# A TensorE loop of 15 rounds, wo in 256 KB pieces, and one VectorE chunk in a decode attention block

## Chip, core, metric

One Trainium2 chip, one core. The metric is the time of one execution on the device in microseconds, as the median over several executions. The kernel before took 670.3 us (median of three runs, 668.88 to 671.2) when the prediction was made. All runs quoted here were in the same (fast) state.

## The reference, cut to what matters

One decode step for two sequences: a layer norm, a q projection, attention over a cache of 8192 keys for 32 heads of 128, the output projection, a residual, and a small ReGLU feed-forward.

```python
B, Sq, D, Hq, Hkv, Sk, Dh, F = 2, 1, 512, 32, 32, 8192, 128, 1376   # all bf16
q = (layernorm(x) @ wq)                            # wq 512 x 4096
scores = einsum("bhqd,bhkd->bhqk", q, k_cache) * Dh ** -0.5
o = einsum("bhqk,bhkd->bhqd", softmax(scores), v_cache)
h = x + o.reshape(B, 1, 4096) @ wo                 # wo 4096 x 512
# h + (relu(g) * u) @ W_down, g and u from layernorm(h) @ W_gate, W_up
```

K and V together are 268 MB, all inputs 281 MB. Nothing is used twice, so the kernel is a stream of loads with arithmetic hidden beside it.

## The kernel before

The 64 (sequence, head) rows are treated as 32 pairs of heads. A pair has one K tile and one V tile of 4 MB. Four slots of 4 MB hold K of two pairs and V of two pairs. For each pair:

- VectorE scores 96 of the 128 key columns that a partition holds, in two chunks of 48: one product, four halving additions, one reduction;
- TensorE transposes the other 32 columns in four groups, ScalarE copies them out of PSUM, and TensorE multiplies them with q;
- ScalarE exponentiates; TensorE multiplies the probabilities with V.

Every engine's program is written out: TensorE's holds 3,187 matmul calls. In the profile a matmul and its weight load are two instructions, and 37 fp32 products stand there as two matmuls each (lines 408 and 319 of the kernel before: 64 and 10 matmuls for 32 and 5 calls), hence 3,224 of each.

```python
# loads: all are issued from one queue (SP), in this order
nc.sync.dma_start(X[:], A_wq.rearrange("(p c) n -> p (c n)", c=DC)).then_inc(sem_wq, 16)
t_k[0] = load(0, slot[0][:], kv(A_k_cache, 0))
# ... v0, k1, v1 into slots 1 to 3
sp.wait(t_q)                                   # X is free once q is there
nc.sync.dma_start(X[:].rearrange("p (h n) -> p h n", n=D),
                  A_wo.rearrange("(h d) n -> d h n", d=128)).then_inc(sem_wo, 16)   # 4 MB in 1 KB rows

for p in range(NP):                            # 32 pairs, cut
    for c in range(NCH):                       # two chunks of 48 columns
        j0, j1 = parts[1 + c]
        dve.wait(t_k[p], t_q_b)
        t_dm = dve.run(nc.vector.tensor_tensor(
            out=prod[:, 0:jc, :], in0=k_t[:, j0:j1, :], in1=qv, op=ALU.mult))
        # ... four tensor_tensor additions (128 -> 8 columns) and a tensor_reduce
        if c == 0:
            pe.wait(t_k[p])
            for g in range(ng):                # four groups of eight key columns
                # ... nc.tensor.transpose x4, ScalarE copy to kT, score_group(p, g - 1)
    if p + 2 < NP:
        sp.wait(t_dm, t_pt[p * NG + ng - 1])   # K slot read by VectorE and by TensorE
        t_k[p + 2] = load(s, slot[s][:], kv(A_k_cache, p + 2))
    if p < NP - 2:
        pv(p)                                  # 32 matmuls, 32 x 512 each
        # ... load_v(p + 2) after pv(p)
```

The softmax here doesn't subtract the row's maximum and nothing guards it: scores larger than these inputs give would overflow.

## Time and profile before

| | |
|---|---|
| time | 670.3 us, profiled execution 669.11 us, span 667.3 us |
| HBM read | 281 MB, 421 GB/s over the span |
| DMA engines | data queue 98.8% of 16 engines' span |
| VectorE / TensorE / ScalarE | 74% / 48% / 32% busy |
| last weights landed | 661.8 us |

These are lines of the page: busy time and share of each engine, the DMA's busy share in 40 slices (tenths), the DMA queues (packets, MB, share of sixteen engines), and the chain of waits that ended last.

```profile
span 667.3 us, 7705 instructions
...
PE 320.9 (48%) x3224; PEld 198.0 (30%) x3224; DVE 490.5 (74%) x433; ACT 211.4 (32%) x535; POOL 5.8 (1%) x17
...
DMA  9999999999999999999999999999999999999995
...
q1 hardware_dynamic: 15600, 281.06, 98.8%
q8 instruction: 25, 0.41, 0.3%
q14 instruction: 9, 0.07, 0.0%
...
DMA 68%; DVE 22%; PE 5%; ACT 3%; issue 1%; SPq 0%; DVEq 0%; ACTq 0%
```

The DMA row has a 9 in every slice but the last. The queues q8 and q14 do not carry data: they carry instructions, 25 packets in q8 (of 16 KB each, by their sizes in the trace) and 9 in q14 within the span (of 8 KB). They are 0.3% of the DMA's time.

Two groups of instructions (line, engine, operation, output<-input, count, then busy us and mean ns, then idle time before them and its cause): the product of 48 columns and the transposes, both waiting for K.

```profile
L433 DVE TENSOR_TENSOR prod<-slot,q_b 128x6144 bf16<-128x6144 bf16 (+1 forms) x64 | 212.8, 3324 | 127.1 <-DMA slot<-in_A_k_cache_dram 124.3
...
L458 PE MATMUL T<-ident_f,slot 128*128 128x128 f32 x528 | 134.7, 422 | 65.4 <-DMA slot<-in_A_k_cache_dram 65.3
```

DMA issues (operation and count, KB each, median us from issue to landing):

```profile
slot<-in_A_k_cache_dram SPq DMA_DIRECT2D x32, 4096.0 KB, 27.7
slot<-in_A_v_cache_dram SPq DMA_DIRECT2D x31, 4096.0 KB, 30.8
...
X<-in_A_wo_dram SPq DMA_DIRECT2D x1, 4096.0 KB, 49.2
```

A load lands 28 to 31 us after its issue, but in the middle of the run the 4 MB loads land 9.7 us apart (300.46, 310.19, 319.90 us). So two loads or more stand in the queue at any time, and an earlier issue alone should gain nothing (tested in e6: K issued 4.9 us sooner, 666.05 us against 665.86).

The end, from the timeline (start us, duration us, engine, line, operation, what it wrote and read, count), cut to the residual sum, the last products and the issue of the output:

```profile
657.49 0.17 DVE L529 TENSOR_TENSOR hb<-W,xlT 128x8 bf16<-128x8 f32 x1 [0.52 <-PE W L352]
...
661.63 1.47 PE L595 MATMUL O<-hd,slot 128*128 128x2 bf16 x40
...
662.96 0.27 PE L595 MATMUL O<-hd,wd_last 96*128 96x2 bf16 x4
...
663.73 0.39 SPq L607 DMA_DIRECT2D out_dram<-o_c  x1
```

and the two W_down loads with their issue and landing times:

```profile
L510 SPq DMA_DIRECT2D slot<-in_B_W_down_dram x2: 434/6450/12466, 634.6 to 635.1; - x2
...
DMA to landing us min/median/max: 25.8/26.3/26.7
```

The second W_down piece was issued at 635.1 us and landed 26.7 us later, at 661.8 us; the last product ended at 663.2 and the span at 667.3.

One more reading is not on the page. Every load here raises its semaphore 16 times, and the trace keeps the time of every increment, but not what made it. They are read here as one from each of the sixteen DMA engines, which the trace does not name. Read so, the spread between the first and the last says how far the engines have drifted apart:

| load of the kernel before, landed at | spread of its 16 increments |
|---|---|
| 24.0 us (K of pair 0) | 1.9 us |
| 230.9 us | 2.0 us |
| 271.2 us | 3.5 us |
| 465.6 us | 3.6 us |
| 505.9 us | 5.0 us |
| 655.1 us (W_up) | 5.1 us |

The 9th instruction packet of q8 started at 262.0 us and the 17th at 499.0 us: just before each step.

The single increments show more. After each of the first eight q8 packets one more of the sixteen comes late: in the loads that landed at 24.0, 43.5, 85.2, 114.4, 143.5, 172.7, 201.8 and 230.9 us, each the first to land after a packet, 1, 2, 3 and so on to 8 increments come 1.7 us or more after the first one. After the 9th packet one of those already late comes 3.5 us after the first, and after the 17th one comes 5.0 us after it. Six increments stay within 0.7 us of the first to the last W_up load, 4.5 to 5.1 us ahead of the latest.

### The profile page before, as it was taken

The numbers are of one execution on the slowest core, as the hardware profiler recorded it, in microseconds if no ns is written. First come the engines' busy times: TensorE is split into PE (matmuls) and PEld (weight loads), VectorE is DVE, ScalarE is ACT, GpSimd is POOL, SyncE is SP. The second block draws the span as 40 slices with busy tenths as digits, with TensorE's granted clock in tenths as the row PEclk, the third lists the DMA queues.
The fourth block names the chain that finished last, engine by engine and source line by source line (L and its number), as shares of the span: only waits on it lengthen the run. The fifth ranks groups of instructions, "written<-read, shape, count | busy, mean of one in ns | idle before, by whom it ended". The sixth has DMA issues, their size and how long they took to land.

```text
span 667.3 us, 7705 instructions
## 1 busy us (share of the span) xinstructions
PE 320.9 (48%) x3224; PEld 198.0 (30%) x3224; DVE 490.5 (74%) x433; ACT 211.4 (32%) x535; POOL 5.8 (1%) x17
## 2 busy tenths in 40 slices
PE   2552353545445434635435553553446564355456
PEld 2330221322223212423213332331224432142336
DVE  1775477797778779777778977777895977788781
ACT  0621222333331323333223333322334142243360
POOL 3000000000000000000000000000000000000000
PEclk9855555555555555555555555555555555555576
DMA  9999999999999999999999999999999999999995
GB/s 377 439 427 364 431 433 423 438 429 431 428 435 428 428 431 437 428 429 430 435 430 431 426 434 428 438 423 432 433 434 426 431 432 428 432 429 434 423 427 203
DMA packets 15638, 281.54 MB, mean 422 GB/s; under 512 B 1426, under 2 KB 6900, under 8 KB 6900
## 3 DMA queue, kind: packets, MB, share of 16 engines
q1 hardware_dynamic: 15600, 281.06, 98.8%
q8 instruction: 25, 0.41, 0.3%
q14 instruction: 9, 0.07, 0.0%
q10 hardware_dynamic: 4, 0.00, 0.0%
HBM read 281.05 MB, written 0.00 MB: 421 GB/s over the span
## 4 chain that ended last, share of the span: by engine, by line
DMA 68%; DVE 22%; PE 5%; ACT 3%; issue 1%; SPq 0%; DVEq 0%; ACTq 0%
DMA slot<-in_A_k_cache_dram 68%; DVE prod L433 14%; DVE tb L441 5%; DVE prod L441 3%; PE T L458 2%; ACT kT L465 2%; DVE scores L448 1%; PE Ob L408 1%; PE S L294 1%; ACT e L304 1%; PE O L392 0%; ACT os_sb L402 0%; PE O L375 0%; PE S L551 0%; PE Ob L319 0%
## 5 line engine op out<-in xcount | busy, mean ns | idle before, releaser
L433 DVE TENSOR_TENSOR prod<-slot,q_b 128x6144 bf16<-128x6144 bf16 (+1 forms) x64 | 212.8, 3324 | 127.1 <-DMA slot<-in_A_k_cache_dram 124.3
L375 PE MATMUL O<-slot,e 128*32 128x512 bf16 x992 | 115.8, 619 | 209.4 <-ACT e L304 133.0
L465 ACT ACTIVATE kT<-T 128x1024 bf16<-128x1024 bf16 x132 | 131.2, 1022 | 165.6 <-PE T L458 161.8
L458 PE MATMUL T<-ident_f,slot 128*128 128x128 f32 x528 | 134.7, 422 | 65.4 <-DMA slot<-in_A_k_cache_dram 65.3
L441 DVE TENSOR_TENSOR tb<-prod 128x3072 bf16<-128x3072 bf16 (+2 forms) x128 | 146.9, 1147 | 4.4
L458 PEld LDWEIGHTS T<-ident_f,slot 128*128 128x128 f32 x528 | 97.2, 217 | 91.9 <-DMA slot<-in_A_k_cache_dram 90.2
L375 PEld LDWEIGHTS O<-slot,e 128*32 128x32 bf16 x992 | 28.4, 127 | 271.8 <-ACT e L304 159.6
L304 ACT ACTIVATE e<-scores 64x48 bf16<-64x48 f32 (+1 forms) x128 | 32.6, 255 | 239.0 <-DVE scores L448 237.2
L441 DVE TENSOR_TENSOR prod<-tb 128x1536 bf16<-128x1536 bf16 (+2 forms) x128 | 83.6, 653 | 4.4
L294 PE MATMUL S<-q,kT 128*128 128x4 bf16 x1056 | 50.1, 169 | 39.2 <-ACT kT L465 39.0
L294 PEld LDWEIGHTS S<-q,kT 128*128 128x128 bf16 x1056 | 43.7, 108 | 69.2 <-ACT kT L465 67.2
L448 DVE TENSOR_REDUCE scores<-prod 128x48 f32<-128x384 bf16 (+1 forms) x64 | 35.1, 549 | 2.3
L304 ACT ACTIVATION_READ_ACCUMULATOR e<-scores 64x1 f32 x128 | 23.6, 185 | 0.0
L408 PE MATMUL Ob<-sel,os_sb 128*128 128x8 f32 x64 | 14.2, 351 | 11.7 <-ACT os_sb L402 11.7
L304 ACT ACTIVATE e<-S 64x32 bf16<-64x32 f32 (+1 forms) x64 | 13.0, 204 | 15.3 <-PE S L294 14.5
L408 PEld LDWEIGHTS Ob<-sel,os_sb 128*128 128x128 f32 x64 | 13.4, 311 | 12.7 <-ACT os_sb L402 12.7
L304 ACT ACTIVATION_READ_ACCUMULATOR e<-S 64x1 f32 x64 | 12.8, 201 | 0.7
L269 ACT ACTIVATE q_b<-O 128x512 bf16<-128x512 f32 x8 | 4.3, 595 | 16.5 <-PE O L264 16.5
L225 DVE CAST qT<-W 128x64 bf16<-128x64 f32 x1 | 0.2, 225 | 11.0 <-PE W L220 11.0
L327 DVE TENSOR_REDUCE zr<-Ob 128x16 f32<-128x48 f32 (+1 forms) x4 | 0.8, 206 | 10.1 <-PE Ob L319 10.1
L220 PE MATMUL W<-xlT,X 128*128 128x2 bf16 x128 | 3.6, 165 | 7.6 <-DMA X<-in_A_wq_dram 7.6
L220 PEld LDWEIGHTS W<-xlT,X 128*128 128x128 bf16 x128 | 3.5, 104 | 7.7 <-DMA X<-in_A_wq_dram 7.7
(69 smaller groups left out, 65.8 us busy)
## 6 DMA issues: line engine op xcount, KB each, us to landing
slot<-in_A_k_cache_dram SPq DMA_DIRECT2D x32, 4096.0 KB, 27.7
slot<-in_A_v_cache_dram SPq DMA_DIRECT2D x31, 4096.0 KB, 30.8
X<-in_A_wq_dram SPq DMA_DIRECT2D x1, 4096.0 KB, 12.2
X<-in_A_wo_dram SPq DMA_DIRECT2D x1, 4096.0 KB, 49.2
slot<-in_A_v_cache_dram SPq DMA_DIRECT2D x2, 2048.0 KB, 28.2
slot<-in_B_W_up_dram SPq DMA_DIRECT2D x1, 1376.0 KB, 21.4
slot<-in_B_W_gate_dram SPq DMA_DIRECT2D x1, 1376.0 KB, 24.3
slot<-in_B_W_down_dram SPq DMA_DIRECT2D x1, 768.0 KB, 25.8
```

The costliest lines, as they stand in the source:

```text
L220: i = nc.tensor.matmul(Wp[:, h * B:(h + 1) * B], lhsT=wq[:, c, h * Dh:(h + 1) * Dh], rhs=lT[:, c * B:(c + 1) * B], start=(c == 0), stop=(c ...
L269: t_cp[m] = act.run(nc.scalar.activation(out=q_b[:, m * 512:(m + 1) * 512], in_=Op[m % 2][:], func=ACT.Copy))
L294: i = nc.tensor.matmul(Sp[p % 2][:, 2 * jj:2 * jj + 4], lhsT=kv_[:, k, r, :], rhs=q2[:, p, r, :], start=(r == 0), stop=(r == 1))
L304: t = act.run(nc.scalar.activation(out=e_t[qd][q, j0 // VJ:j1 // VJ, 8 * qd:8 * qd + 8].rearrange("p g (j a) -> p g j a", a=2)[:, :, :, a] ...
L327: dve.run(nc.vector.tensor_reduce(out=zr[:, 2 * p0:2 * p1], in_=zbank(k)[:, zcol(k):zcol(k) + n * (NCH + 1)].rearrange("p (n k) -> p n k", ...
L375: i = nc.tensor.matmul(Op[gr % 2][c:c + 32, :], lhsT=e_t[qd][:, j // VJ, :], rhs=v_t[:, j:j + VJ, :].rearrange("p j d -> p (j d)"), start= ...
L408: i = nc.tensor.matmul(Ob[:, 2 * p0:2 * p0 + 2 * PG], lhsT=os_sb[:, jj * Dh:(jj + 1) * Dh], rhs=sel[:, 2 * PG * jj:2 * PG * jj + 2 * PG], ...
L433: t_dm = dve.run(nc.vector.tensor_tensor(out=prod[:, 0:jc, :], in0=k_t[:, j0:j1, :], in1=qv, op=ALU.mult))
L441: dve.run(nc.vector.tensor_tensor(out=o, in0=cur[:, :, 0:half], in1=cur[:, :, half:w], op=ALU.add))
L448: t_s = dve.run(nc.vector.tensor_reduce(out=sc[:, 0:jc], in_=cur, axis=AX.X, op=ALU.add))
L458: i = nc.tensor.transpose(Tp[n % 2][:, k * 128:(k + 1) * 128], k_t[:, j:j + 2, :].rearrange("p j d -> p (j d)").bitcast(F32), ident_f[:])
L465: t_ev[n] = act.run(nc.scalar.activation(out=kT[n % 2][:], in_=Tp[n % 2][:].bitcast(BF16), func=ACT.Copy))
```

## The change

Intent: make TensorE's program short. The 30 first pairs become 15 rounds of a loop whose body handles two pairs with fixed addresses and fixed semaphore counts. That has consequences: q of the pair has to be copied to a fixed place (by POOL), wo must be at a fixed place too and so comes as 256 KB for each round, the X tile of 4 MB goes (wq uses slot 3), and the freed memory holds VectorE's working tiles for all its 96 columns in one chunk. The diff, cut to its core:

```diff
-    NCH = 2
-    JC = (J - NG * GT) // NCH
+    JC = J - NG * GT
-    PG = 4
+    PG = 2
+    NI = NP // 2 - 1
-        X = sb("X", [128, H * D], BF16)
+        wo_cur = sb("wo_cur", [128, 2 * D], BF16)
+        wo_last = sb("wo_last", [128, 2 * D], BF16)
+        q2c = [sb(f"q2c{i}", [128, 2, 4], BF16) for i in range(2)]
 ... cut ...
+                with nc.Fori(0, NI, engines=OrderedEngineSet([nc.tensor.engine])):
+                    jd = split(0)[1]
+                    k_part(body, 0, 0, ((g2p, 1),))
+                    collect(body, 6)
+                    pv(body, 0, ((jd, J, ((v2p, 1), (a2p, 5))), (0, jd, ((a2p, 7),))))
+                    k_part(body, 1, 7, ((g2p, 2),))
+                    nc.tensor.wait_ge(d2p, 1)
+                    nc.tensor.wait_ge(v2p, 2)
+                    o_proj(body, wo_cur, 0, B)
+                    nc.tensor.sem_inc(d2p, -1)
+                    pv(body, 1, ((jd, J, ((v2p, 3), (a2p, 12))), (0, jd, ((a2p, EV),))))
+                    z_sum(body, Ob)
+                    nc.tensor.sem_inc(g2p, -2)
+                    nc.tensor.sem_inc(v2p, -3)
+                    nc.tensor.sem_inc(a2p, -EV)
 ... cut: two pairs and the last products written out after the loop ...
+                    if p < P0:
+                        nc.gpsimd.wait_ge(slot_sem[s], 16 * (g + 1))
+                    nc.gpsimd.tensor_copy(out=q2c[p % 2][:], in_=q2[:, p]).then_inc(g2p, 1)
 ... cut ...
-                    for c in range(NCH):
-                        j0, j1 = parts[1 + c]
-                        dve.wait(t_k[p], t_q_b)
+                    dve.wait((slot_sem[s], 16 * (g + 1)), t_q_b)
+                    t_dm[p] = dve.run(nc.vector.tensor_tensor(
+                        out=prod[:, 0:jd, :], in0=k_t[:, 0:jd, :], in1=qv, op=ALU.mult))
 ... cut ...
+                    if p % 2 == 1 and 1 <= g < NI:
+                        sp.wait(tok("om", g))
+                        load_wo(wo_cur, g, sem_wo)
```

In the built programs TensorE has 6,415 instructions before and 1,468 after: 357 ahead of the loop, 355 in its body, 752 after it, and four at the program's two ends (a matmul call counted as two, fp32 doublings not counted). The 25 packets for 6,415 instructions are about 257 a packet; the blocks of 256 instructions in the prediction are this estimate.

## The prediction

> **What bounds the kernel.** The DMA. In the page's slices the sixteen DMA engines are 90% or more busy from the first slice to the last but one; the queue table gives 98.8% to the data queue, 281 MB at 422 GB/s. In the chain of waits 68% is the K loads. VectorE is 74% busy, TensorE 48%; both wait for K in every 19.4 us pair. At the end, the last weight piece lands at 661.8 us and the span ends 5.5 us later.
>
> **Where DMA time is lost.** The trace holds the sixteen completion increments of every load. Their spread is 1.9 us on the first K load, 2.0 at 230 us, 3.6 from 270 us, 5.1 from 510 us: six engines end 4.5 to 5 us before the slowest. The steps follow the instruction queue: 25 packets of 16 KB, one about every 28 us, 1.0 to 1.1 us each; the 9th and the 17th make the steps. So TensorE's instruction blocks seem to be fetched over eight of the engines in turn, each fetch setting its engine back about 1.5 us, and a load lands with its slowest engine. That costs about 4.4 us at the end.
>
> **What the change does.**
> 1. The TensorE loop: 3,224 matmuls with as many weight loads become about 900 pairs of program text. The body is about 365 instructions, two blocks. [...] nothing in this trace shows a branch. If the blocks stay, some 5 to 8 fetches are left, the slowest engine gains about 3 us. If each round fetches two or three blocks again, there are 35 to 50: spread over eight engines about 0 to +4 us, on the same two or three engines about +17 us (estimate: 15 x 1.45 less 4.4). [...]
> 2. wo in pieces: same 1 KB packets (348 GB/s between 54 and 64 us, against about 437), so the same loss, spread out: 0 to +0.5.
> 3. One 96-column chunk: the product takes about 6.6 us instead of two of 3.36; K slots come free about 4.5 us sooner, V slots at the same time (probabilities after about 15 us either way). The queue holds two loads already: about 0.
> 4. Tail: the last pair's P.V uses wide matmuls; the copy, selection and scaling add about 2.5 us after it but 128 narrow matmuls go. Attention ends 1 to 2 us earlier, hidden behind the weights' landing.
>
> **On the critical path:** only the fetches (item 1) and the tail's DMA end. Likely sum: -3 + 0.5 = about -2.5 us.
>
> **Predicted: 667.5 us, 80% range 663 to 682.** Faster by over 2%: 0.02; within 2%: 0.84; slower by over 2%: 0.14.
>
> **What would show it.** Instruction packets fall from 25 to under 10; the spread of the last loads' increments falls from 5.1 to about 2 to 3 us; the last weight lands near 659 us and the span ends 5 to 6 us later; DMA busy stays about 99%; K issue to landing grows from 27.7 to about 32 us.
>
> **What would make it wrong.** More instruction packets than before (refetch each round), worst if they sit on few engines: spread over 10 us, pair period over 19.6 us. Or gaps in the DMA slices, if slots come free late (the even pair's start after the branch, or the relay through POOL).

"If the blocks stay" is an assumption. About -3 us for item 1 under that assumption, at most +0.5 for item 2 and about 0 for items 3 and 4 come to -2.5 us. From 670.3 us that is 667.8; the 667.5 is 0.3 us lower, and the text does not say why.

## The result, and the profile after

The changed kernel takes **665.86 us** (median of four runs, 665.75 to 666.0) against 670.75 us for the kernel before in the same comparison (median of four, 668.88 to 671.74). The ratio is 0.993, 95% interval 0.9908 to 0.9953: the same at 2%, but clearly 0.7% faster. Ratios here are the mean time of one kernel's fast runs over that of the other's of the same rounds, so not quite the ratio of the medians. The measured time lies inside the forecast range; the gain was 4.9 us between the medians instead of the forecast 2.8 from 670.3.

The same lines of the page:

```profile
span 664.0 us, 7589 instructions
...
PE 339.3 (51%) x3223; PEld 220.8 (33%) x3223; DVE 465.7 (70%) x275; ACT 198.5 (30%) x416; POOL 194.1 (29%) x48
...
DMA  9999999999999999999999999999999999999996
...
q1 hardware_dynamic: 15840, 281.06, 99.2%
q8 instruction: 5, 0.08, 0.0%
q14 instruction: 7, 0.06, 0.0%
...
DMA 71%; DVE 26%; PE 1%; ACT 0%; issue 0%; SPq 0%; DVEq 0%
```

The instruction packets of TensorE went from 25 to 5, as forecast, and q14 from 9 to 7. The data queue's share rose to 99.2%: the same bytes in less time. The chain now holds W_down's landing (5% in the full listing), so the end is closer to the data.

The groups that answer to those of before, and the costliest one, which is new:

```profile
L455 POOL COPY q2c<-q 128x8 bf16<-128x8 bf16 x32 | 190.3, 5947 | 417.2 <-DMA slot<-in_A_k_cache_dram 359.6
L466 DVE TENSOR_TENSOR prod<-slot,q_b 128x12288 bf16<-128x12288 bf16 (+1 forms) x32 | 207.7, 6492 | 130.4 <-DMA slot<-in_A_k_cache_dram 128.8
L325 PE MATMUL T<-ident_f,slot 128*128 128x128 f32 x528 | 136.5, 426 | 219.3 <-POOL q2c L455 217.0
```

POOL's copy of eight numbers a partition takes 5.9 us on average, and TensorE's transposes now wait for it (217.0 of their 219.3 us of idle time) instead of for K.

The issues:

```profile
slot<-in_A_k_cache_dram SPq DMA_DIRECT2D x32, 4096.0 KB, 28.1
slot<-in_A_v_cache_dram SPq DMA_DIRECT2D x31, 4096.0 KB, 31.6
...
wo_cur<-in_A_wo_dram SPq DMA_DIRECT2D x15, 256.0 KB, 27.1
```

K's time from issue to landing hardly moved (27.7 to 28.1 us); the forecast had said about 32. The middle of the run shows why, in the timeline around one pair, whose K landed at 321.42 us:

```profile
321.45 6.56 DVE L466 TENSOR_TENSOR prod<-slot,q_b 128x12288 bf16<-128x12288 bf16 x1 [2.55 <-DMA slot<-in_A_k_cache_dram]
321.55 6.51 POOL L455 COPY q2c<-q 128x8 bf16<-128x8 bf16 x1 [12.94 <-DMA slot<-in_A_k_cache_dram]
...
328.11 1.97 PE L325 MATMUL T<-ident_f,slot 128*128 128x128 f32 x8 [6.29 <-POOL q2c L455]
...
332.90 0.33 SPq L158 DMA_DIRECT2D slot<-in_A_k_cache_dram  x1
```

VectorE's product starts at once. POOL's copy starts 0.1 us after it and ends when the product ends; only then TensorE's first transpose starts. The K slot waits for the last transpose, and K is issued 11.5 us after the landing, as late as before the change (about 11.2 us).

The end, from the timeline, the same steps as shown of before:

```profile
652.78 0.17 DVE L545 TENSOR_TENSOR hb<-W,xlT 128x8 bf16<-128x8 f32 x1 [0.52 <-PE W L366]
...
659.42 0.67 PE L611 MATMUL O<-hd,slot 128*128 128x2 bf16 x16 [0.33 <-DMA slot<-in_B_W_down_dram]
...
659.95 0.27 PE L611 MATMUL O<-hd,wd_last 96*128 96x2 bf16 x4
...
660.72 0.39 SPq L623 DMA_DIRECT2D out_dram<-o_c  x1
```

and the two W_down loads with their issue and landing times:

```profile
L527 SPq DMA_DIRECT2D slot<-in_B_W_down_dram x2: 433/9390/18346, 626.6 to 627.1; - x2
...
DMA to landing us min/median/max: 31.4/31.8/32.2
```

The last weights were issued at 627.1 and landed 32.2 us later, at 659.3 us: 2.5 us earlier than before. The residual sum is made at 652.8 us instead of 657.5, the last product ends at 660.2, 0.9 us after the landing instead of 1.4, and the span ends 4.7 us after the landing instead of 5.5.

The drift of the engines, from the completion increments:

| | before | after |
|---|---|---|
| spread, first K load | 1.9 us | 1.8 us |
| spread, K load landed at 465.6 us (460.4 after) | 3.6 us | 2.0 us |
| spread, W_up | 5.1 us | 2.4 us |
| last weights' last increment | 661.8 us | 659.3 us |
| last weights' first increment | 657.0 us | 657.1 us |

The last row is the telling one. If each increment is one engine's, the fastest engine finished its share at the same time in both kernels (657.0 and 657.1 us), and only the slow ones got faster.

### The profile page after: what moved, and what is told of

It reads as the page before. It is cut to its first block, busy times and chain, and to the rows that moved or that the text cites. A ratio compares the mean times of both kernels' runs of the same rounds, so it can differ in the third digit from the quotient of the medians.

```text
span 664.0 us, 7589 instructions
## 1 busy us (share of the span) xinstructions
PE 339.3 (51%) x3223; PEld 220.8 (33%) x3223; DVE 465.7 (70%) x275; ACT 198.5 (30%) x416; POOL 194.1 (29%) x48
## 3 DMA queue, kind: packets, MB, share of 16 engines
q1 hardware_dynamic: 15840, 281.06, 99.2%
## 4 chain that ended last, share of the span: by engine, by line
DMA 71%; DVE 26%; PE 1%; ACT 0%; issue 0%; SPq 0%; DVEq 0%
DMA slot<-in_A_k_cache_dram 64%; DVE prod L466 16%; DVE tb L474 7%; DMA slot<-in_B_W_down_dram 5%; DVE prod L474 3%; DMA slot<-in_A_wq_dram 2%; PE W L229 1%; ACT q_b L276 0%; PE O L271 0%; DVE q L249 0%; PE O L611 0%; SPq L523 0%; SPq L527 0%; DVE tb L262 0%; PE S L240 0%
## 5 line engine op out<-in xcount | busy, mean ns | idle before, releaser
L455 POOL COPY q2c<-q 128x8 bf16<-128x8 bf16 x32 | 190.3, 5947 | 417.2 <-DMA slot<-in_A_k_cache_dram 359.6
L466 DVE TENSOR_TENSOR prod<-slot,q_b 128x12288 bf16<-128x12288 bf16 (+1 forms) x32 | 207.7, 6492 | 130.4 <-DMA slot<-in_A_k_cache_dram 128.8
L325 PE MATMUL T<-ident_f,slot 128*128 128x128 f32 x528 | 136.5, 426 | 219.3 <-POOL q2c L455 217.0
L474 DVE TENSOR_TENSOR tb<-prod 128x6144 bf16<-128x6144 bf16 (+1 forms) x64 | 136.8, 2137 | 2.2
L474 DVE TENSOR_TENSOR prod<-tb 128x3072 bf16<-128x3072 bf16 (+1 forms) x64 | 73.4, 1148 | 2.2
L313 PE MATMUL S<-q2c,kT 128*128 128x4 bf16 x1056 | 50.4, 170 | 37.7 <-ACT kT L491 37.7
L313 PEld LDWEIGHTS S<-q2c,kT 128*128 128x128 bf16 x1056 | 44.1, 108 | 67.8 <-ACT kT L491 65.9
L353 PE MATMUL Ob<-sel,os_sb 128*128 128x4 f32 x136 | 31.0, 351 | 26.3 <-ACT os_sb L499 25.6
L353 PEld LDWEIGHTS Ob<-sel,os_sb 128*128 128x128 f32 x136 | 29.5, 320 | 28.1 <-ACT os_sb L499 26.9
L479 DVE TENSOR_REDUCE scores<-prod 128x96 f32<-128x768 bf16 (+1 forms) x32 | 30.2, 945 | 1.1
L423 ACT ACTIVATE e<-scores 64x96 bf16<-64x96 f32 (+1 forms) x64 | 19.6, 307 | 22.8 <-DVE scores L479 22.0
L432 DVE TENSOR_REDUCE zr<-Ob 128x4 f32<-128x8 f32 x15 | 2.5, 166 | 28.1 <-PE Ob L353 28.1
## 6 DMA issues: line engine op xcount, KB each, us to landing
slot<-in_A_k_cache_dram SPq DMA_DIRECT2D x32, 4096.0 KB, 28.1
```

Of the source, the lines that this page charges most:

```text
L313: i = nc.tensor.matmul(Sp[p % 2][:, 2 * jj:2 * jj + 4], lhsT=kv_[:, k, r, :], rhs=q2c[p % 2][:, r, :], start=(r == 0), stop=(r == 1))
L325: i = nc.tensor.transpose(Tp[g % 2][:, k * 128:(k + 1) * 128], k_t[:, j:j + 2, :].rearrange("p j d -> p (j d)").bitcast(F32), ident_f[:])
L353: i = nc.tensor.matmul(Ob[:, 0:4], lhsT=os_sb[:, jj * Dh:(jj + 1) * Dh], rhs=sel[:, 4 * jj:4 * jj + 4], start=(jj == 0), stop=(jj == VJ - 1))
L423: i = nc.scalar.activation(out=e_t[q][h, j0 // VJ:j1 // VJ, 8 * q:8 * q + 8].rearrange("p g (j a) -> p g j a", a=2)[:, :, :, a], in_=src(h ...
L455: nc.gpsimd.tensor_copy(out=q2c[p % 2][:], in_=q2[:, p]).then_inc(g2p, 1)
L466: t_dm[p] = dve.run(nc.vector.tensor_tensor(out=prod[:, 0:jd, :], in0=k_t[:, 0:jd, :], in1=qv, op=ALU.mult))
```

## The experiments

Theory A, to be tested: an instruction fetch goes through one of the sixteen DMA engines, sets it back, and a load lands with its slowest engine. Rivals: B, the single VectorE chunk or wo in pieces gave the time; C, the new end of the program did. Unless said otherwise an edit is made to the changed kernel, whose own time of 665.86 us is the comparison. Every result below was correct against the reference. The changed kernel was timed in one job and the experiments in three others, on chips 0, 3 and 6. On chips 3 and 6 three programs with few packets (e3, e6, e9) came out at 665.9 to 666.05 us, so the comparison carries over. On chip 0 (e1, e2, e2b, e5) only the kernel before stands beside them, with a median of 670.95 us against 670.75 in the first job.

### e1_unrolled: the loop written out again

```diff
-                with nc.Fori(0, NI, engines=OrderedEngineSet([nc.tensor.engine])):
+                for _round in range(NI):
-                n_body = pe.count - body.base
+                n_body = (pe.count - body.base) // NI
```

(and the bookkeeping keeps the first round's places). Expected:

> The changed kernel with the TensorE loop written out 15 times and nothing else changed (same waits, same counters, same order). Theory A (instruction fetches set single DMA engines back): instruction packets of 16 KB go from 5 back to about 25, the spread of the last weight's completion increments from 2.4 to about 5 us, the last weight lands near 662 us instead of 659.3, time 668 to 670 us. Theory B (the gain comes from wo in pieces, or from the one VectorE chunk): stays at 666 us, whatever the packets do. Theory C (the gain comes from the new end of the program): stays at 666 us.

Measured: 669.88 us (669.48 to 670.28, five runs), ratio to before 0.9985 (0.9967 to 1.0003). The instruction packets are back in the queue table of this run:

```profile
q1 hardware_dynamic: 15840, 281.06, 98.8%
q8 instruction: 25, 0.41, 0.3%
q14 instruction: 7, 0.06, 0.0%
```

W_up's spread is 5.15 us and the last weights landed at 663.1 us. So with the same waits, the same wo pieces and the same single chunk, writing the loop out costs 4.0 us, and that is most of the gain. Theory A's numbers all came. B and C are left about the 1.1 us between the medians of this kernel and the one before, which is not clear of noise: the interval holds no difference at all, and at its other end 0.33%, or 2.2 us. In the traces the new end (C) is a little shorter: the span ends 4.6 us after the last landing here and 5.5 in the kernel before.

In the profiled run, about 1 us of the 4.0 is a matter of timing. The 25th packet came at 660.2 us, during the last load, whose landing followed the one before by 2.4 us and not by 1.3 as in the kernel before and the changed one. In the profiled run of the kernel before, the 25th packet came at 662.3 us, after the last landing.

### e3_loop5x3 and e4_loop3x5: how long a loop may be

```diff
-                with nc.Fori(0, NI, engines=OrderedEngineSet([nc.tensor.engine])):
-                    jd = split(0)[1]
+                with nc.Fori(0, NI // 3, engines=OrderedEngineSet([nc.tensor.engine])):
+                    for _u in range(3):
+                        jd = split(0)[1]
                     # ... the body as it was, one level deeper; e4 has 5 for 3
```

> The same program with three rounds written out in the loop's body, which runs five times: 1,061 instructions, a little over four blocks of 256. [...] about 8 instruction packets in all, 666 to 667 us. [...] each of five passes fetches four or five again, 25 packets or more and 669 to 671 us.

> Five rounds written out, three passes: 1,767 instructions, about seven blocks, touching eight. [...] about 11 packets, 666 to 667 us. [...] about 7 packets a pass, 25 or so in all, and 668.5 to 670 us, as with the loop written out.

The outcomes stand in this order: the body's text stays from one pass to the next, or it is fetched again in each.

Measured: the five passes of 1,061 instructions took 665.9 us with 8 instruction packets in all and W_up's spread at 2.1 us: as fast as the short loop. The three passes of 1,767 instructions took 669.96 us, as slow as the program written out, with W_up's spread at 6.7 us and the last weights landed at 663.2 us:

```profile
q8 instruction: 29, 0.48, 0.3%
```

So five passes over 1,061 instructions (a little over four packets' worth) came with 8 packets in all, and three passes over 1,767 (about seven) with 29. With 8 packets in five passes, the second outcome of e3, text fetched again in each pass, is out; in e4 it is the second outcome that fits, with 29 packets for the 25 or so expected. The trace does not show which blocks were fetched, nor why. e4 is also a second confirmation of theory A: the loop is there, the packets are there, the gain is not.

### e2_unrolled_double and e2b_loop_padded: a dose that failed

178 instructions that only wait on a passed semaphore were put after each pair, in the written-out kernel and in the loop.

```diff
+                def pad():
+                    for _ in range(356):                 # two waits go into one instruction
+                        nc.tensor.wait_ge(sem_x, 16)
                     pv(body, 0, ((jd, J, ((v2p, 1), (a2p, 5))), (0, jd, ((a2p, 7),))))
+                    pad()
 ... and after z_sum(body, Ob)
```

> The written-out kernel with 178 instructions that only wait on a semaphore long passed added after each pair, so that the TensorE text goes from about 6,400 to 11,700 instructions. Theory A: about 46 instruction packets, five or six on each of eight engines instead of three; about 3 more a slowest engine at 1.45 us each, so the spread goes to about 9 to 10 us and the time to 672 to 675 us. Theories B and C: 666 us. TensorE has several us to spare in a pair, so the added waits alone should cost nothing; the padded loop is the control.

> Control: the same added waits in the loop, whose body then is 710 instructions, three to four blocks of 256. All theories: 666 us if the added waits cost nothing and the loop's blocks stay on the chip (about 6 to 8 instruction packets). If blocks behind the current one are given up, each of the 15 rounds fetches about three blocks again: some 50 packets and 670 us or more.

Measured: 925.2 and 927.11 us. The filler was far from free: in the trace TensorE stood still for 16.1 us over one filler of 178 instructions, 90 ns for an instruction with two waits, which made TensorE the bottleneck. These two runs say nothing on theory A by their times. They still gave two facts: the control's 710-instruction body needed 7 instruction packets in all, and the written-out program had 46, as forecast, with a W_up spread of only 1.9 us. There the data queue is busy for 73.2% and not 99%; whether that is why the drift did not pile up from load to load was not tested.

### e8_unrolled_dummies and e9_loop_dummies: the dose with a cheap filler

```diff
+                def pad():
+                    for _ in range(90):
+                        nc.tensor.matmul(Op[1][:, 200:202], lhsT=ident[:], rhs=zero[:, 0:2], start=True, stop=True)
 ... called at the same two places; e8 with the loop written out, e9 in the loop
```

(A first form that wrote to the bank Ob was refused by the race check, in both kernels: VectorE reads that bank at the same time. It did not run.)

> The dose again, with a cheap filler: the written-out kernel with 90 dummy matmuls (two columns, into a PSUM bank nobody reads) after each pair; about 11,800 TensorE instructions instead of 6,400. They should fit into the wait for the next K (about 8 us). Theory A: about 46 instruction packets, the spread of the last loads near 9 us, 672.5 to 675 us. If instruction fetches did nothing, 670 us as without the fillers.

> Control: the same 90 dummy matmuls a pair in the loop (body 715 instructions, under three blocks). Theory A: 7 to 8 instruction packets, spread 2 to 3 us, 666 to 666.7 us. If the fillers' own time costs something, it shows here.

Measured: e9, the control, 665.92 us with 7 packets, W_up's spread 2.3 us: the fillers cost nothing (90 of them take about 2.5 us, in TensorE's idle time). e8, 672.93 us, ratio to before 1.0038 (1.0023 to 1.0054):

```profile
q8 instruction: 46, 0.75, 0.5%
```

The same arithmetic and the same fillers, 39 packets more, 7.0 us more. Against e1 (25 packets, 669.88 us) the 21 added packets cost 3.1 us. The answer to the dose is plain: 5, 25 and 46 packets give 665.9, 669.9 and 672.9 us.

This trace also shows the turn of eight most clearly. The spread makes five steps, each between one load and the next: 1.8 to 3.2 us, 3.4 to 4.7, 4.9 to 6.2, 6.5 to 7.7 and 8.0 to 9.1. Just before them came the 9th, 17th, 25th, 33rd and 41st packet (141.6, 248.5, 365.2, 478.7 and 588.0 us). If every eighth packet adds a step, from the first on, e8 has six and e1 four; two more at about 1.5 us are an estimate of 3.0 us, close to the 3.1 measured.

The spread reached 9.4 us, as expected, in the load that landed at 626.3 us, and fell to 7.1 in the next. The first increment of the load at 626.3 had come at 616.8 us, 0.5 us before the next K load was issued (617.3 us). That the engines ahead then had nothing to do and lost a part of their lead is the author's reading of these two times. W_up's spread was left at 7.2 us.

### e5_two_chunks: VectorE's two chunks back

```diff
-                        out=prod[:, 0:jd, :], in0=k_t[:, 0:jd, :], in1=qv, op=ALU.mult))
+                    for c0 in (0, jc):                    # jc = jd // 2
+                        t_dm[p] = dve.run(nc.vector.tensor_tensor(
+                            out=prod[:, 0:jc, :], in0=k_t[:, c0:c0 + jc, :], in1=qv, op=ALU.mult))
                         # ... the additions and the reduction of each chunk
```

> The changed kernel with VectorE's 96 columns again as two chunks of 48. Theory A: VectorE is about 0.8 us busier in a pair and the time stays at 666 us within 0.5. Theory B (one chunk gives the gain): back to about 670 us.

Measured: 667.8 us (667.56 to 668.14, five runs), 1.9 us slower. That was outside the 0.5 us that theory A was given, and not the 670 of B. TensorE still had 5 packets; but q14 had 9 packets of 8 KB instead of 7, VectorE ran 467 instructions instead of 275, and W_up's spread was 4.1 us. It had stepped from 3.0 to 4.0 after a packet of 8 KB at 596.8 us. So a new form of theory A: the fetches of VectorE's own instructions do the same harm. That needed its own test.

### e10_dve_text: more VectorE text, little more VectorE time

```diff
+                    for x in range(24):
+                        dve.run(nc.vector.memset(junk[:, x:x + 1], 0.0))
```

> The changed kernel with 24 one-column memsets more on VectorE in each pair (768 instructions, six blocks of 8 KB), on a tile that nobody reads. They fit into VectorE's wait for K (4 us or more). If two VectorE chunks cost 1.9 us because of VectorE's own instruction fetches (8 KB each): about 13 packets of 8 KB instead of 7, spread up by 1 to 4 us, 667 to 669 us. If the second chunk cost its time in another way, 666 us.

Measured: 671.54 us (671.13 to 671.9), ratio to before 1.0018: 5.7 us slower than the changed kernel, more than the 1 to 4 expected. The memsets of a pair take 0.55 us, in VectorE's wait for K. The queues:

```profile
q8 instruction: 5, 0.08, 0.0%
q14 instruction: 13, 0.11, 0.0%
```

Six packets of 8 KB more. The spread of the loads rises by 0.9 to 1.0 us after each of those at 201, 281, 361, 442, 522 and 602 us: 2.1, 3.1, 4.1, 5.0, 6.0, 7.0, 8.0 us (6.7 for W_up at the end, after the same fall as in e8). They add up one on the other: here each of the six packets (records of about 0.3 us) made a step, while of TensorE's 16 KB packets (1.0 to 1.1 us) it took eight to make one of about 1.5 us. Packets at 43 and 122 us, in the same rhythm of 80 us, fit this: after each, one increment came about 1 us later against the others. Not all of q14 need be VectorE's: packets at 82, 282 and 483 us stand at nearly the same places in the changed kernel (82, 280 and 479 us). So a packet that came with VectorE's text was dearer here than one of TensorE's: 5.7 us for six, about 1 us each, against 4.0 us for 20, or 0.2 us.

### e6_copy_early: POOL's copy before K lands

```diff
-                    if p < P0:
-                        nc.gpsimd.wait_ge(slot_sem[s], 16 * (g + 1))
-                    nc.gpsimd.tensor_copy(out=q2c[p % 2][:], in_=q2[:, p]).then_inc(g2p, 1)
+                    nc.gpsimd.tensor_copy(out=q2c[p % 2][:], in_=q2[:, p]).then_inc(q2d, 1)
+                    nc.gpsimd.wait_ge(q2d, p + 1)
+                    if p < P0:
+                        nc.gpsimd.wait_ge(slot_sem[s], 16 * (g + 1))
+                    nc.gpsimd.sem_inc(g2p, 1)
```

> The changed kernel with POOL's copy of the query columns made before the K tile lands, not after it; only the counter that releases TensorE still waits for K. In the changed kernel that copy takes 6.5 us because VectorE's long product runs beside it, and TensorE's transposes and with them the K slot wait for it. Expected: the transposes start within 0.5 us of the K landing instead of 6.6 us after it, K is issued 6.6 us after the landing instead of 11.5, K issue to landing grows from 28.1 to about 33 us, and the time stays at 666 us within 0.5, because the DMA queue always holds two loads. If a freed slot's earlier refill is worth anything (rival), 1 us or more faster.

Measured: 666.05 us, ratio to before 0.9924, the same as the changed kernel. Everything in the schedule moved as expected, shown by the timeline of one pair:

```profile
341.27 6.56 DVE L468 TENSOR_TENSOR prod<-slot,q_b 128x12288 bf16<-128x12288 bf16 x1 [5.83 <-DMA slot<-in_A_k_cache_dram]
...
341.33 1.97 PE L325 MATMUL T<-ident_f,slot 128*128 128x128 f32 x8 [1.77 <-POOLq L457]
...
347.86 0.33 SPq L158 DMA_DIRECT2D slot<-in_A_k_cache_dram  x1
...
351.12 0.19 POOL L453 COPY q2c<-q 128x8 bf16<-128x8 bf16 x1 [18.20 <-PE Ob L353]
```

TensorE's transposes start with VectorE's product, K is issued 6.6 us after the start instead of 11.5, and K's median time from issue to landing is 33.0 us instead of 28.1. POOL's copy had a mean of 0.7 us instead of 5.9. And none of it is worth anything, because the queue was never short of loads: in the changed kernel the 4 MB loads already land 9.7 us apart (341.56, 351.29, 361.02 us), K's 28.1 us after its issue. The copy's length had gone with VectorE's product beside it: in the changed kernel the copy of 6.51 us ends 0.05 us after the product that started at 321.45 us and took 6.56; in e5 a copy beside a product of 3.36 us took 3.31; and in this run, away from the product, a copy takes 0.2 to 1.6 us. What holds the copy up is not shown.

### e7_before_pieces: the kernel before, with wo in pieces

```diff
-                nc.sync.dma_start(X[:]..., A_wo...).then_inc(sem_wo, 16)
+                def load_wo(g): ...                     # 256 KB, heads 2g and 2g + 1, into its part of X
                         t_k[p + 2] = load(s, slot[s][:], kv(A_k_cache, p + 2))
+                    if p < 16:
+                        load_wo(p)
```

> The kernel before with wo loaded in sixteen pieces of 256 KB, one after the K load of each of the first sixteen pairs, and nothing else. Theory A: the same 1 KB packets cost the same in sum, the 25 instruction packets stay: 670 to 671 us as before. Theory B (the one long wo load of 12 us at 348 GB/s, and the SP queue held up behind it, cost the time): 667 us or less.

Measured: 670.87 us, ratio to before 0.9999 (0.9979 to 1.0019). The 25 packets and a spread of 5.4 us stayed. Pieces alone show no effect; the interval leaves them at most 1.4 us either way.

### e11_longer_runs: an attempt at a better kernel

The small rows of wo and W_down were lengthened, by letting a partition hold neighbouring rows.

```diff
-  A_wo[...].rearrange("(h d) n -> d h n", d=128)          # 1 KB rows
+  A_wo[...].rearrange("(p h) n -> p h n", h=2)            # 2 KB a partition
-  B_W_down[r0 * 128:r1 * 128].rearrange("(r p) n -> p r n", p=128)
+  B_W_down[0:1280].rearrange("(p r) n -> p r n", r=10)[:, r0:r1, :]
-  lhsT=w[:, c, f * 128:f * 128 + fw]                       # W_up, W_gate
+  lhsT=w[:, c, 0:1280].rearrange("p (q r) -> p r q", r=10)[:, f, :]   # every tenth column
 ... O is gathered and scaled in two halves of 64 partitions to match
```

> The changed kernel with wo and W_down loaded in longer runs: wo as 2 KB for each partition of a round (rows 2p and 2p+1; O is put on the partitions to match), W_down as 6 and 4 KB for each partition instead of 1 KB rows. If a 1 KB packet costs about 9.5 ns more of an engine's time than its bytes at the full rate (47 against 37.5 ns, from 348 and 437 GB/s), half of wo's 2.4 us and most of W_down's 0.76 us come back: 664 to 664.5 us. If not, 666 us. TensorE has 8 more small products a round, off the path.

Measured: 666.48 us (666.05 to 668.1), no gain. The DMA did what was expected: the two-pair period fell from 39.6 to 39.53 us, and the last weights landed at 657.5 us, 1.8 us earlier. But the end no longer followed them. W_up and W_gate are now read with a step of ten columns, and the weight loads became slower. In the changed kernel (line and operation, then minimum, median and maximum in ns):

```profile
L567 PEld LDWEIGHTS S<-d_b,slot x44: 95/96/125, 653.5 to 654.6; 128*128 128x128 bf16 x40, 128*96 128x96 bf16 x4
L567 PE MATMUL S<-d_b,slot x44: 163/163/183, 653.5 to 654.7; 128*128 128x2 bf16 x40, 128*96 128x2 bf16 x4
```

and here:

```profile
L580 PEld LDWEIGHTS S<-d_b,slot x44: 137/158/196, 654.3 to 656.9; 128*128 128x128 bf16 x40, 128*96 128x96 bf16 x4
L580 PE MATMUL S<-d_b,slot x44: 197/197/219, 654.3 to 656.9; 128*128 128x2 bf16 x40, 128*96 128x2 bf16 x4
```

The 44 products took 2.81 us instead of 1.33, W_gate's followed late, and the span ended 7.9 us after the last landing instead of 4.7. The step of ten is the obvious difference, but it was not tried alone. No run was made with wo's longer rows only.

## Why the prediction was right, and where it was off

- **What bounds the kernel: right.** DMA at 99% in both, and every experiment that added or moved work of TensorE or POOL, or moved the loads of wo, with at most two instruction packets more (e6, e7, e9) left the time within 0.2 us of its kernel. The forecast range also holds the time of the kernel before, so that 665.86 us lies in it proves little; the forecasts of the next point prove more.
- **The drift of the engines and its cause: right.** Forecast: under 10 packets, spread 2 to 3 us, last weights near 659 us. Measured: 5, 2.4, 659.3. e1 restored all three together with the time, and e8 gave more of each.
- **"the slowest engine gains about 3 us": right, a little small.** e1 measures the term at 4.0 us between medians (663.1 to 659.3 us for the last landing), with about 1 us of it from the one late packet.
- **"If the blocks stay": settled for the lengths that were run.** A body of 355 instructions came with 5 packets in all and one of 1,061 with 8 (e3); one of 1,767 came with 29 (e4). The prediction's 5 to 8 packets held; the cases with text fetched again in each round, which made up its long upper range, did not come here, but e4 shows one of them a step away.
- **wo in pieces, 0 to +0.5: right.** The two-pair period rose from 38.85 to 39.6 us, 0.75 us for a piece of 256 KB that needs 0.60 at 437 GB/s (an estimate; 437 is the rate in most slices of 1.2 us between 620 and 640 us of the kernel before); 15 times 0.15 is the 2.3 us that the one long load had lost. e7: no difference.
- **One chunk, "about 0": wrong.** It was costed as work off VectorE's path, which it is. What it also takes away is VectorE program text (467 instructions to 275, 9 packets of q14 to 7), and e5 measures 1.9 us for the second chunk in the looped kernel. The prediction had read q8 and had not asked who q14 belonged to. This is the term of the sum that was most mis-sized, and it was given 0. It shows where TensorE's fetches are gone: with all 25 of them, W_up's spread is 5.1 us with one chunk (e1) as with two (the kernel before).
- **"K slots come free about 4.5 us sooner": wrong, and worthless.** POOL's new copy waited for VectorE's product, and K was issued as late as before. e6 made it come true, and the time stayed.
- **Tail: right in size, hidden mostly.** Attention ended 4.7 us earlier, but 2.6 us of this is that the last piece of V landed earlier (649.1 us instead of 651.8); the tail itself became 2.1 us shorter (forecast 1 to 2). About 0.8 us came through: the span ends 4.7 instead of 5.5 us after the last landing, which the forecast had left as it was.

The terms do not simply add, since by theory A they all act on whichever engine is last. Between the medians, the kernel written out with one chunk is 1.1 us faster than the kernel before (not clear of noise), and the loop takes off the other 4.0.

Some things stay open. The runs of the kernel before scatter over 3.6 us (668.88 to 672.49 in all jobs) and those of the changed kernel over 0.25; the cause is not known. Fewer fetches do not explain it: e1, e4 and e8, with 25, 29 and 46 packets, scatter over 0.8, 0.4 and 0.7 us, while e7, the kernel before with wo in pieces, scatters over 2.6. Only one run of each was traced. The profiled run of before, 669.11 us, was one of its fast ones, which is why the spans differ by 3.3 us and the medians by 4.9. And one q8 packet of the changed kernel came at 300.8 us, in the middle of the loop, with no cause that the trace shows; in e5, e6 and e10, whose TensorE program is the same, the third packet came at 66.5, 340.4 and 142.4 us. Why each of e10's six packets made a step and only every eighth of TensorE's did is not shown either; the trace does not name the engines.

## What to carry to other kernels

In this kernel, with the DMA 99% busy, the program's own text was traffic: 25 instruction packets instead of 5 cost 4.0 us, and 46 cost 7.0. In another one like it, count the packets of the instruction queues, and look at the spread of a load's sixteen completion increments (5.1 us before, 2.4 after), not only at the mean busy share (98.8% and 99.2%). A long unrolled program can be shortened by a loop (a body of 1,061 instructions came with 8 packets here, one of 1,767 with 29) or by fewer, larger instructions on the other engines (one chunk instead of two on VectorE: 1.9 us), even where those engines are idle a quarter of the time, as VectorE was at 74% busy. Making slots free sooner was worth nothing while the queue already held two loads (e6: 666.05 us).
